# A shared ScalarE copy for q and k, a rotating pair of PSUM banks for the x transpose, and GpSimd-built sink rows in a fused attention and highway kernel

## The chip, the cores and the metric

The kernel runs on one core of one Trainium2 chip. The metric is the device time of one execution in microseconds (us). The kernel before had a median of 137.3 us when it was handed over, and of 137.55 us over four runs. The profiles show the span of one execution on the core, which is about 1.7 us shorter than the timed figure of the same run. Here "slow" means only a run that was over 1.5% above the fastest of its kernel, and all ratios use fast runs alone; a median that is quoted is over all runs of its kernel.

## The reference, cut to what matters

```python
# q, k, v: (4 batches, 8 heads, 768 positions, 64)
scores = q @ k.T / 8
keep   = (pos_k < 4) | ((pos_q - pos_k >= 0) & (pos_q - pos_k < 128))  # 4 sink rows + window of 128
a      = softmax(where(keep, scores, -1e9))
x      = (a @ v) laid out as (3072 tokens, 512)
H = max(x @ w_h, 0);  T = sigmoid(x @ w_t + b_t)
out = T * H + (1 - T) * x
```

The kernel cuts the 3072 tokens into 24 blocks of 128, six to a batch. A block's scores need the keys of the block itself and of the block before (except for a batch's first block), and, from a batch's third block on, the four sink rows. I call the work from x to out "the highway". Its two products are "the t matmuls" (x times w_t, opened by a matmul that adds the bias) and "the h matmuls" (x times w_h).

## The kernel before

The start: the columns of ones that give the softmax denominator (they hold 2.0 in the code, so that xh is half of x, which the last steps make up for) are set before the loads, for the first three v buffers, and the others inside the loop, each just before its v load is issued. All loads are issued by GpSimd and cast fp32 to fp16.

```python
def init_v(vt):
    nc.vector.memset(vt[:, 0:H * 65].rearrange("p (h e) -> p h e", e=65)[:, :, D:D + 1], 2.0)
    nc.vector.memset(vt[:, H * 65:VW], 0.0)

for vt in v_ring[0:3]:
    init_v(vt)
...
    load(0); ...; load_v(0); load(1); ...; load_v(1); ...; load(2)
    nc.gpsimd.dma_start(out=wt_sb, in_=moe_w_t...)
    load_v(2)
    load(3)
    nc.gpsimd.dma_start(out=wh_sb, in_=moe_w_h...)
```

The program uses eight PSUM banks: two score buffers of two banks each, one av buffer of two, and the pool `m_ps` with two one-bank buffers. The x transpose shares the av buffer. The q and k transposes share one bank of `m_ps`, and two engines copy them out:

```python
def stage_T(n):
    tp = m_ps.tile([P, 2 * NHP, P], FP16, tag="m", name="tp")
    ...                                            # 8 TensorE transposes
    nc.scalar.copy(out=qT, in_=tp[:, 0:NHP, :])
    nc.vector.tensor_copy(out=kT, in_=tp[:, NHP:2 * NHP, :])

def stage_X(n):
    xtp = av_ps.tile([P, NOC, P], FP16, tag="av", name="xtp")
    ...
```

The main loop (cut to its order; the program order on TensorE, VectorE and ScalarE is exactly this):

```python
for i in range(-2, NB + 1):
    s = i + 1
    stage_sink(i)        # sink scores, for two blocks at once
    stage_S(s)           # scores and exp, two halves
    stage_A(i)           # attention times v (AV), reciprocal, xh
    stage_T(i + 2)       # and, at a batch's first block, 10 small DMAs for the sink rows
    load(...); init_v(...); load_v(...)
    stage_mask(s)        # two mask multiplies
    stage_Mt(i - 1); stage_X(i); stage_Mh(i - 1)   # highway, one block behind
```

The softmax here doesn't subtract the row's maximum and nothing guards it: scores larger than these inputs give would overflow.

Of the kernel before, what the change touches and what calls it, by code (L numbers as in the profile page):

```python
# [20 lines left out]
def kernel(  # L21
# [26 lines left out]
    assert 1 <= NSINK <= 4  # L48
# [10 lines left out]
    AHEAD = 8  # L59

# [4 lines left out]
    es_pool = ctx.enter_context(tc.tile_pool(name="p_es", bufs=2))  # L65
    r_pool = ctx.enter_context(tc.tile_pool(name="p_r", bufs=3))
    x_pool = ctx.enter_context(tc.tile_pool(name="p_x", bufs=4))
# [6 lines left out]
    NV = AHEAD + 3  # L74
# [3 lines left out]
    def load(n):  # L78
        b, c = divmod(n, NSC)
        rows = slice(c * P, (c + 1) * P)  # L80
        qsd = sd_pool.tile([P, H, D], FP16, tag="qsd", name="qsd")
        ksd = sd_pool.tile([P, H, D], FP16, tag="ksd", name="ksd")
        nc.gpsimd.dma_start(out=qsd, in_=q[b, :, rows, :].transpose([1, 0, 2]))  # L83
        nc.gpsimd.dma_start(out=ksd, in_=k[b, :, rows, :].transpose([1, 0, 2]))  # L84
        qk_sd[n] = (qsd, ksd)
# [7 lines left out]

    warm = const.tile([P, DM], FP16, tag="warm")
    nc.vector.memset(warm, 0.0)
    ident = const.tile([P, P], FP16, tag="ident")
    nc.vector.memset(ident, 1.0)
    ebias = const.tile([P, 1], FP32, tag="ebias")
    nc.vector.memset(ebias, _EXP_BIAS)
    mask = const.tile([P, 2, P], FP16, tag="mask", name="mask")  # L100
    nc.vector.memset(mask, 1.0)

    def init_v(vt):

        nc.vector.memset(vt[:, 0:H * 65].rearrange("p (h e) -> p h e", e=65)[:, :, D:D + 1], 2.0)
        nc.vector.memset(vt[:, H * 65:VW], 0.0)

    for vt in v_ring[0:3]:
        init_v(vt)
    wh_sb = const.tile([P, NOC, DM], FP16, tag="wh")  # L110
    wt_sb = const.tile([P, NOC, DM], FP16, tag="wt")

    with tc.manual_schedule(engines={ENG.Pool}):
        load(0)
# [4 lines left out]
        load(1)  # L119

# [7 lines left out]
        load(2)  # L128
        nc.gpsimd.dma_start(out=wt_sb, in_=moe_w_t.rearrange("(kc p) of -> p kc of", p=P))
        load_v(2)  # L130
        load(3)
        nc.gpsimd.dma_start(out=wh_sb, in_=moe_w_h.rearrange("(kc p) of -> p kc of", p=P))


    bt32 = const.tile([1, DM], FP32, tag="bt32")
    nc.sync.dma_start(out=bt32, in_=moe_b_t.unsqueeze(0))
    bt16 = const.tile([P, DM], FP16, tag="bt16")
    nc.vector.memset(bt16, 0.0)
    ones_row = const.tile([P, P], FP16, tag="ones_row")
    nc.vector.memset(ones_row, 0.0)  # L140
    nc.vector.memset(ones_row[0:1, :], 1.0)
    mask0 = const.tile([P, P], FP16, tag="mask0", name="mask0")
    mask1 = const.tile([P, 2, P], FP16, tag="mask1", name="mask1")


    ks_bd, vs_bd = [], []
    for i in range(2):
        t = const.tile([P, NHP * 160], FP16, tag=f"ks{i}", name=f"ks{i}")
        nc.vector.memset(t, 0.0)
        ks_bd.append(t)  # L150
        t = const.tile([P, 2, 4, 65], FP16, tag=f"vs{i}", name=f"vs{i}")
        nc.vector.memset(t, 0.0)
        vs_bd.append(t)

    def warm_up(n):

        w = m_ps.tile([P, DM], FP32, tag="m", name="wps")
        for _ in range(n):
            nc.tensor.matmul(w, lhsT=warm[:, 0:P], rhs=warm, start=True, stop=True)

    def late_constants():

# [5 lines left out]


    qkT = {}  # L170
    e_of = {}
    es_of = {}
    xh_of = {}
    xT_of = {}

    def stage_T(n):
# [6 lines left out]
        qT = qkT_pool.tile([P, NHP, P], FP16, tag="qT", name="qT")  # L183
        kT = qkT_pool.tile([P, NHP, P], FP16, tag="kT", name="kT")
        nc.scalar.copy(out=qT, in_=tp[:, 0:NHP, :])  # L185
        nc.vector.tensor_copy(out=kT, in_=tp[:, NHP:2 * NHP, :])  # L186
        qkT[n] = (qT, kT)

    def stage_sink_setup(b):

        _, kT = qkT[b * NSC]
        ks3 = ks_bd[b % 2].rearrange("p (a b) -> p a b", b=160)
        for hh in range(2):
            rows = slice(64 * hh, 64 * hh + 64)
            nc.sync.dma_start(out=ks3[rows, :, 4 * hh:4 * hh + NSINK],
                              in_=kT[rows, :, 0:NSINK])
        vt = v_ring[(b * NSC) % NV]
        for h in range(H):
            r = 32 * (h // 2) + 4 * (h % 2)
            nc.sync.dma_start(out=vs_bd[b % 2][r:r + NSINK, h // 4, h % 4, :],  # L200
                              in_=vt[0:NSINK, 65 * h:65 * h + 65])

    def stage_sink(n):

        b = n // NSC
        ks = ks_bd[b % 2]
# [6 lines left out]
        es = es_pool.tile([P, 2, P], FP16, tag="es", name="es")  # L213
        nc.scalar.activation(out=es, in_=sk, func=AF.Exp, bias=ebias, scale=SCALE)
        es_of[n] = es_of[n + 1] = es

    def stage_S(n):
        c = n % NSC
        qT, kT = qkT[n]
        srcs = ([] if c == 0 else [qkT[n - 1][1]]) + [kT]  # L220
        np_ = len(srcs)
        es = []
        for g in range(2):
            sps = s_ps.tile([P, 2, 512], FP32, tag="s", name="sps")
            for hl in range(2):
                hp = 2 * g + hl
                for pc, kk in enumerate(srcs):
                    for hh in range(2):
                        rows = slice(64 * hh, 64 * hh + 64)
                        o = (hl * np_ + pc) * P  # L230
                        nc.tensor.matmul(sps[:, hh, o:o + P], lhsT=kk[rows, hp, :],  # L231
                                         rhs=qT[rows, hp, :], start=True, stop=True)
            e = e_pool.tile([P, 2, 2, np_, P], FP16, tag="e", name="e")
            nc.scalar.activation(out=e.rearrange("p a b c d -> p a (b c d)"),  # L234
                                 in_=sps[:, :, 0:2 * np_ * P], func=AF.Exp,
                                 bias=ebias, scale=SCALE)
            es.append(e)
        e_of[n] = (es, np_)

    def stage_mask(n):  # L240
        c = n % NSC
        es, np_ = e_of[n]
        m = {0: mask0, 1: mask1.rearrange("p a b -> p (a b)")}.get(
            c, mask.rearrange("p a b -> p (a b)"))
        for e in es:
            ev = e.rearrange("p a b c d -> p (a b) (c d)")
            nc.vector.tensor_tensor(  # L247
                out=ev, in0=ev, in1=m.unsqueeze(1).to_broadcast([P, 4, np_ * P]),
                op=ALU.mult)

    def stage_A(n):
        b, c = divmod(n, NSC)
        es, np_ = e_of.pop(n)
        vts = ([] if c == 0 else [v_ring[(n - 1) % NV]]) + [v_ring[n % NV]]
        av = av_ps.tile([P, 2, 4, P], FP32, tag="av", name="av")
        for g in range(2):
            first = True
            for hl in range(2):
                for hh in range(2):
                    h = 2 * (2 * g + hl) + hh  # L260
                    for pc, vt in enumerate(vts):
                        nc.tensor.matmul(  # L262
                            av[:, g, 2 * hl + hh, 0:_AVN], lhsT=es[g][:, hh, hl, pc, :],
# [3 lines left out]
            if c >= 2:  # L267
                nc.tensor.matmul(
                    av[:, g, :, 0:65], lhsT=es_of[n][:, c % 2, :],
                    rhs=vs_bd[b % 2][:, g, :, :], start=False, stop=True,  # L270
                    skip_group_check=True)
        es_of.pop(n, None)
        avh = av.rearrange("p g h e -> p (g h) e")
        rec = r_pool.tile([P, H], FP32, tag="rec", name="rec")
        nc.vector.reciprocal(out=rec.unsqueeze(2), in_=avh[:, :, 64:65])
        xh = x_pool.tile([P, H, D], FP16, tag="xh", name="xh")
        nc.vector.tensor_tensor(  # L277
            out=xh, in0=avh[:, :, 0:D],
            in1=rec.unsqueeze(2).to_broadcast([P, H, D]), op=ALU.mult)
        xh_of[n] = xh  # L280

    def stage_X(n):
        xh = xh_of[n]
        xtp = av_ps.tile([P, NOC, P], FP16, tag="av", name="xtp")
        for j in range(NOC):
            nc.tensor.transpose(xtp[:, j, :], xh[:, 2 * j:2 * j + 2, :], ident)  # L286
        xT = x_pool.tile([P, NOC, P], FP16, tag="xT", name="xT")
        nc.scalar.copy(out=xT, in_=xtp)  # L288
        xT_of[n] = xT

    u_of = {}

    def stage_Mt(n):
# [3 lines left out]
        for kc in range(NOC):  # L297
            nc.tensor.matmul(tps, lhsT=xT[:, kc, :], rhs=wt_sb[:, kc, :],  # L298
                             start=False, stop=(kc == NOC - 1))
        u = td_pool.tile([P, DM], FP16, tag="u", name="u")  # L300
        nc.scalar.activation(out=u, in_=tps, func=AF.Tanh)  # L301
        u_of[n] = u

    def stage_Mh(n):
        xT = xT_of.pop(n)
        xh = xh_of.pop(n).rearrange("p h d -> p (h d)")
        u = u_of.pop(n)
        hps = m_ps.tile([P, DM], FP32, tag="m", name="hps")
        for kc in range(NOC):
            nc.tensor.matmul(hps, lhsT=xT[:, kc, :], rhs=wh_sb[:, kc, :],  # L310
                             start=(kc == 0), stop=(kc == NOC - 1))
        dd = td_pool.tile([P, DM], FP16, tag="dd", name="dd")
        nc.vector.scalar_tensor_tensor(out=dd, in0=hps, scalar=0.0, in1=xh,  # L313
                                       op0=ALU.max, op1=ALU.subtract)
        ee = td_pool.tile([P, DM], FP16, tag="ee", name="ee")
        nc.vector.scalar_tensor_tensor(out=ee, in0=u, scalar=1.0, in1=dd,  # L316
                                       op0=ALU.add, op1=ALU.mult)
        otok = o_pool.tile([P, DM], FP32, tag="otok", name="otok")
        nc.vector.scalar_tensor_tensor(out=otok, in0=xh, scalar=2.0, in1=ee,  # L319
# [3 lines left out]
    with tc.manual_schedule(engines={ENG.PE, ENG.DVE, ENG.Activation}):  # L323
        for i in range(-2, NB + 1):
            s = i + 1
            if 0 <= i < NB and i % NSC >= 2 and i % 2 == 0:
                stage_sink(i)
            if 0 <= s < NB:
                stage_S(s)
# [60 lines left out]
```

## Time and profile before

| | kernel before |
|---|---|
| median of 4 runs | 137.55 us (136.64 to 137.91) |
| span in the profile | 134.9 us |
| first AV / third AV / last AV start | 12.82 / 25.3 / 122.7 us |
| steady period of six blocks | 28.13 us, 4.69 a block |

The profile's first part gives each engine's busy time, its share of the span, and the instruction count. PE is TensorE, PEld its weight loads, DVE VectorE, ACT ScalarE and POOL GpSimd.

```profile
PE 117.1 (87%) x1312; PEld 73.6 (55%) x1312; DVE 108.5 (80%) x230; ACT 90.4 (67%) x129; POOL 65.7 (49%) x81
```

Its second part cuts the span in 40 slices; a digit is the busy share in tenths, and the PEclk row is TensorE's granted clock in tenths.

```profile
PE   6657939999999899999999899999998999999720
DVE  6153724789988999899898998998989998999590
PEclk9999995999999999999999999999999999999996
```

The windows view of the stretch from 30 to 110 us gives its length, then the busy time of PE, PEld, DVE, ACT and POOL (instruction counts in brackets), the clock, the DMA share and GB/s.

```profile
30.00:110.00 80.00, 76.82 (x929) 49.41 (x928) 73.64 (x138) 63.04 (x92) 41.23 (x48) 1.00 1.51 143
```

So in the steady stretch TensorE is 96% busy and VectorE 92%. Which of the two sets the pace is not told by those shares, since matmuls overlap one another (the AV matmuls last 0.21 us each and start 0.05 us apart). The timeline of VectorE tells more. Its columns are start, duration, engine, line, operation, what is written from what, and the count; a bracket at the end is the idle time before and what released it. The first line here is from one batch earlier.

```profile
37.76 1.28 DVE L247 TENSOR_TENSOR e<-e,mask 128x1024 f16<-128x1024 f16 x2
...
65.55 0.42 DVE L186 COPY kT<-tp 128x512 f16<-128x512 f16 x1 [0.40 <-ACT qT L185]
65.89 1.28 DVE L247 TENSOR_TENSOR e<-e,mask 128x1024 f16<-128x1024 f16 x2
67.09 0.69 DVE L313 SCALAR_TENSOR_TENSOR dd<-hps,xh 128x512 f16<-128x512 f32 x1
67.88 0.69 DVE L316 SCALAR_TENSOR_TENSOR ee<-u,dd 128x512 f16<-128x512 f16 x1
68.61 0.69 DVE L319 SCALAR_TENSOR_TENSOR otok<-xh,ee 128x512 f32<-128x512 f16 x1
69.22 0.20 DVE L275 RECIPROCAL rec<-av 128x8 f32<-128x8 f32 x1
69.45 0.69 DVE L277 TENSOR_TENSOR xh<-av,rec 128x512 f16<-128x512 f32 x1
```

The same mask multiply starts at 37.76 and 65.89 us, which is the period of 28.13 us. Inside a block VectorE goes from one instruction to the next, apart from one wait of 0.40 to 0.45 us in three of the six blocks (for the q copy, as here, or for the h matmuls), and these lines are the budget that the change was to cut.

Three places in the timeline of TensorE: the first AV, the first sink scores with the third AV, and the last AV (v_91 and so on are buffer names).

```profile
12.82 0.93 PE L262 MATMUL av<-v_91,e 128*128 128x112 f16 x8
...
24.22 0.61 PE L211 MATMUL sk<-qT,ks_154 128*128 128x128 f16 x8
...
25.32 0.22 PE L262 MATMUL av<-v_92,e 128*128 128x112 f16 x1
...
122.69 0.21 PE L262 MATMUL av<-v_91,e 128*128 128x112 f16 x1
```

Two groups of the profile's list of costliest groups are the copies in question (total busy, mean ns of one, then idle time before them and its releaser):

```profile
L185 ACT COPY qT<-tp 128x512 f16<-128x512 f16 x24 | 14.0, 585 | 9.6 <-PE tp L182 9.6
L186 DVE COPY kT<-tp 128x512 f16<-128x512 f16 x24 | 10.1, 423 | 11.7 <-ACT qT L185 11.7
```

The k copy waits for the q copy. Both read one PSUM bank, from two engines. The Trainium skill (PSUM — Partial Sum Buffer, "PSUM bank collisions raise a hardware error") says that two engines must not touch one bank (in the same partitions) at once, readers included, and that the guard should go by bank and 32-partition quadrant, or simply by bank; here the program makes the second copy wait, and this group waited 11.7 us in all. Most of that lies at the start: in the two batches from 45 to 101 us it was 1.6 us.

### The profile page before, as it was taken

How to read it: one execution, taken by the hardware profiler on the slowest of the kernel's cores; microseconds unless marked ns; L12 is line 12 of the kernel's file. 1: busy time of each engine (PE TensorE's matmuls, PEld its weight loads, DVE VectorE, ACT ScalarE, POOL GpSimd, SP SyncE). 2: the span in 40 equal slices, each digit the busy share in tenths (PEclk: the TensorE clock that was granted, in tenths of full speed). 3: DMA queues.
4: the chain of work that ended last, by engine and by line, in shares of the span. 5: the costliest groups of instructions: out<-in, count | busy, mean ns of one | idle time of the engine just before them, and what ended most of it. 6: DMA issues, size and time to landing. Idle time of an engine off the chain costs nothing.

```text
span 134.9 us, 3378 instructions
## 1 busy us (share of the span) xinstructions
PE 117.1 (87%) x1312; PEld 73.6 (55%) x1312; DVE 108.5 (80%) x230; ACT 90.4 (67%) x129; POOL 65.7 (49%) x81
## 2 busy tenths in 40 slices
PE   6657939999999899999999899999998999999720
PEld 2225625856864466567565557656653685665300
DVE  6153724789988999899898998998989998999590
ACT  3054843779775977977777788779767977973310
POOL 6999747889897789979489370000000000000000
PEclk9999995999999999999999999999999999999996
DMA  0999999999999999999999999122011101101111
GB/s 4 111 123 127 160 188 160 155 181 171 154 198 191 196 151 148 152 195 240 192 194 179 193 194 176 38 80 80 6 78 78 63 19 78 78 5 78 78 78 78
DMA packets 81841, 17.02 MB, mean 126 GB/s; under 512 B 77729, under 2 KB 78753, under 8 KB 81826
## 3 DMA queue, kind: packets, MB, share of 16 engines
q0 software_dynamic: 75936, 10.49, 116.0%
q1 hardware_dynamic: 5890, 6.33, 14.6%
q8 instruction: 10, 0.16, 0.5%
q14 instruction: 5, 0.04, 0.1%
HBM read 20.97 MB, written 6.29 MB: 202 GB/s over the span
## 4 chain that ended last, share of the span: by engine, by line
DVE 33%; PE 32%; ACT 11%; issue 8%; POOL 7%; DMA 6%; DVEq 0%; POOLq 0%
PE hps L310 12%; ACT e L234 7%; DMA ksd<-in_k_dram 6%; DVE ee L316 6%; DVE otok L319 6%; DVE dd L313 6%; DVE e L247 5%; DVE xh L277 5%; PE tps L298 4%; PE xtp L286 4%; PE av L262 3%; DVE kT L186 3%; PE sk L211 3%; ACT qT L185 3%; POOL qsd L83 2%
## 5 line engine op out<-in xcount | busy, mean ns | idle before, releaser
L234 ACT ACTIVATE e<-sps,ebias 128x1024 f16<-128x1024 f32 (+1 forms) x48 | 47.4, 1039 | 11.2 <-PE sps L231 6.0
L298 PE MATMUL tps<-wt_sb,xT 128*128 128x512 f16 x96 | 25.5, 390 | 0.0
L310 PE MATMUL hps<-wh_sb,xT 128*128 128x512 f16 x96 | 24.7, 379 | 0.7
L83 POOL DMA_DIRECT2D qsd<-in_q_dram x24 | 21.6, 900 | 4.7 <-DMA wh_sb<-in_moe_w_h_dram 1.0
L84 POOL DMA_DIRECT2D ksd<-in_k_dram x24 | 21.4, 893 | 3.1 <-PE tp L182 1.3
L262 PEld LDWEIGHTS <-e 128*128 128x128 f16 x352 | 19.8, 98 | 3.2 <-issue 0.4
L301 ACT ACTIVATE u<-tps 128x512 f16<-128x512 f32 x24 | 14.4, 600 | 9.5 <-PE tps L298 9.5
L247 DVE TENSOR_TENSOR e<-e,mask 128x1024 f16<-128x1024 f16 x32 | 20.5, 682 | 0.0
L185 ACT COPY qT<-tp 128x512 f16<-128x512 f16 x24 | 14.0, 585 | 9.6 <-PE tp L182 9.6
L313 DVE SCALAR_TENSOR_TENSOR dd<-hps,xh 128x512 f16<-128x512 f32 x24 | 16.5, 688 | 4.1 <-PE hps L310 4.1
L186 DVE COPY kT<-tp 128x512 f16<-128x512 f16 x24 | 10.1, 423 | 11.7 <-ACT qT L185 11.7
L316 DVE SCALAR_TENSOR_TENSOR ee<-u,dd 128x512 f16<-128x512 f16 x24 | 16.6, 692 | 2.5
L319 DVE SCALAR_TENSOR_TENSOR otok<-xh,ee 128x512 f32<-128x512 f16 x24 | 16.6, 692 | 0.8
L277 DVE TENSOR_TENSOR xh<-av,rec 128x512 f16<-128x512 f32 x24 | 16.6, 691 | 0.8
L231 PE MATMUL sps<-qT,kT 64*128 64x128 f16 x352 | 15.4, 227 | 2.1 <-DVE kT L186 1.1
L231 PEld LDWEIGHTS <-kT 64*128 64x128 f16 x352 | 10.7, 98 | 9.5 <-issue 6.6
L288 ACT COPY xT<-xtp 128x512 f16<-128x512 f16 x24 | 14.0, 583 | 1.1 <-PE xtp L286 0.9
L298 PEld LDWEIGHTS <-xT 128*128 128x128 f16 x96 | 9.6, 100 | 9.1 <-issue 0.8
L310 PEld LDWEIGHTS <-xT 128*128 128x128 f16 x96 | 9.3, 98 | 8.6 <-issue 1.5
L286 PEld LDWEIGHTS <-xh 128*128 128x128 f16 x96 | 6.4, 101 | 13.4 <-DVE xh L277 11.2
L286 PE MATMUL xtp<-ident,xh 128*128 128x128 f16 x96 | 9.9, 228 | 3.8 <-DVE xh L277 3.8
L180 PE MATMUL tp<-ident,qsd 128*128 128x128 f16 x96 | 10.0, 231 | 2.4 <-DMA qsd<-in_q_dram 2.3
(88 smaller groups left out, 152.9 us busy)
## 6 DMA issues: line engine op xcount, KB each, us to landing
out_dram<-otok SPq DMA_DIRECT2D x24, 256.0 KB
qsd<-in_q_dram POOLq DMA_DIRECT2D x24, 128.0 KB, 7.3
ksd<-in_k_dram POOLq DMA_DIRECT2D x24, 128.0 KB, 7.4
wt_sb<-in_moe_w_t_dram POOLq DMA_DIRECT2D x1, 512.0 KB, 8.4
wh_sb<-in_moe_w_h_dram POOLq DMA_DIRECT2D x1, 512.0 KB, 10.1
v_91<-in_v_dram POOLq DMA_DIRECT2D x3, 128.0 KB, 8.0
v_92<-in_v_dram POOLq DMA_DIRECT2D x3, 128.0 KB, 6.1
v_93<-in_v_dram POOLq DMA_DIRECT2D x2, 128.0 KB, 8.0
```

What stands on the lines that cost most here:

```text
L83: nc.gpsimd.dma_start(out=qsd, in_=q[b, :, rows, :].transpose([1, 0, 2]))
L231: nc.tensor.matmul(sps[:, hh, o:o + P], lhsT=kk[rows, hp, :], rhs=qT[rows, hp, :], start=True, stop=True)
L234: nc.scalar.activation(out=e.rearrange("p a b c d -> p a (b c d)"), in_=sps[:, :, 0:2 * np_ * P], func=AF.Exp, bias=ebias, scale=SCALE)
L247: nc.vector.tensor_tensor(out=ev, in0=ev, in1=m.unsqueeze(1).to_broadcast([P, 4, np_ * P]), op=ALU.mult)
L262: nc.tensor.matmul(av[:, g, 2 * hl + hh, 0:_AVN], lhsT=es[g][:, hh, hl, pc, :], rhs=vt[:, 65 * h:65 * h + _AVN], start=first, stop=False, ...
L277: nc.vector.tensor_tensor(out=xh, in0=avh[:, :, 0:D], in1=rec.unsqueeze(2).to_broadcast([P, H, D]), op=ALU.mult)
L286: nc.tensor.transpose(xtp[:, j, :], xh[:, 2 * j:2 * j + 2, :], ident)
L298: nc.tensor.matmul(tps, lhsT=xT[:, kc, :], rhs=wt_sb[:, kc, :], start=False, stop=(kc == NOC - 1))
L310: nc.tensor.matmul(hps, lhsT=xT[:, kc, :], rhs=wh_sb[:, kc, :], start=(kc == 0), stop=(kc == NOC - 1))
L313: nc.vector.scalar_tensor_tensor(out=dd, in0=hps, scalar=0.0, in1=xh, op0=ALU.max, op1=ALU.subtract)
L316: nc.vector.scalar_tensor_tensor(out=ee, in0=u, scalar=1.0, in1=dd, op0=ALU.add, op1=ALU.mult)
L319: nc.vector.scalar_tensor_tensor(out=otok, in0=xh, scalar=2.0, in1=ee, op0=ALU.mult, op1=ALU.add)
```

## The change

The intent: take work from VectorE (the k copy moves into one 1024-wide ScalarE copy), reorder VectorE's instructions so that dependent ones don't stand next to each other, take the x transpose out of the av buffer so that the next AV needn't wait for it, run the highway two blocks behind so that its inputs are always ready, and replace ten small DMAs per batch for the sink rows by GpSimd work (two copies for k, and for v a multiply that is fed by one small load). The diff cut to its core (long renamings into one function per engine are left out):

```diff
-    NV = AHEAD + 3
+    LAG = 2
+    NV = AHEAD + 4
 ...
+        load_qk(2)
+        ...                                  # two selects that build bm, the head pattern
+        load_v(2)
+        load_sink_v(0)
+        load_qk(3)
+        load_v(3)
         nc.gpsimd.dma_start(out=wt_sb, in_=moe_w_t...)
-        load_v(2)
-        load(3)
         nc.gpsimd.dma_start(out=wh_sb, in_=moe_w_h...)
+        load_qk(4)
+        load_v(4)
 ...
-        nc.scalar.copy(out=qT, in_=tp[:, 0:NHP, :])
-        nc.vector.tensor_copy(out=kT, in_=tp[:, NHP:2 * NHP, :])
+        qk = qkT_pool.tile([P, 2 * NHP, P], FP16, tag="qk", name="qk")
+        nc.scalar.copy(out=qk, in_=tp_of.pop(n))
 ...
-            nc.sync.dma_start(out=ks3[rows, :, 4 * hh:4 * hh + NSINK], in_=kT[rows, :, 0:NSINK])
+            nc.gpsimd.tensor_copy(out=dst[:, :, 4 * hh:4 * hh + NSINK], in_=kT[rows, :, 0:NSINK])
-        for h in range(H):                   # v sink rows, 8 DMAs
-            nc.sync.dma_start(out=vs_bd[...][...], in_=vt[0:NSINK, 65 * h:65 * h + 65])
+        nc.gpsimd.tensor_tensor(out=vs_bd[b % 2][0:NS4, :, 0:D], in0=vs_dn..., in1=bm..., op=ALU.mult)
 ...
-        xtp = av_ps.tile([P, NOC, P], FP16, tag="av", name="xtp")
+        xtp = m_ps.tile([P, NOC, P], FP16, tag="m", name="xtp")
```

The new loop, with the checks for the ends cut away:

```python
for i in range(-2, NB + LAG + 1):
    m, o = i - LAG, i - LAG - 1
    if i == -2:
        warm_up(8); more_constants(); late_constants()
        for vt in v_ring[3:NV]: init_v(vt)          # after the loads of v blocks 3 and 4 are issued
        sink_ones(); sink_v(0)
    act_sink(i); pe_S(i + 1, 0); act_S(i + 1, 0); pe_S(i + 1, 1)
    dve_d(o); dve_mask(i, 1)
    pe_T(i + 2); pe_X(i - 1); dve_e(o); pe_A(i)
    act_T(i + 2); act_X(i - 1)
    act_S(i + 1, 1); dve_mask(i + 1, 0); dve_rec(i); dve_o(o); dve_x(i)
    pe_Mt(m); act_u(m); pe_Mh(m); pe_sink(i + 1)
    for n in ((5 .. AHEAD) if i == -2 else (i + 2 + AHEAD)): load_qk(n); load_v(n)
    if (i + 2) % NSC == 0: pool_sink((i + 2) // NSC)   # k sink copies, on GpSimd, behind the loads
    if i % NSC == 3: load_sink_v(i // NSC + 1)
    if i % NSC == 0 and i > 0: sink_v(i // NSC)
```

## The prediction

> **What bounds the kernel now.** In steady state VectorE. The timeline repeats every 28.13 us per batch of six blocks (mask multiplies at 37.84, 65.97, 94.11), 4.69 us per block. The windows view from 30 to 110 us gives VectorE 92% busy, TensorE 96% (pipelined, not its limit), ScalarE about 79%. Start to start on VectorE: k copy 0.34, masks 1.20, dd 0.79, ee 0.73, otok 0.61, reciprocal 0.23, xh 0.6: about 4.5. Start-up is loads: block 3 is transposed at 19.5, the third block's attention-times-v (AV) starts at 25.3, the last block's AV at 122.7, and the span ends at 134.9.
>
> **Removed, added, moved, per block.**
> - VectorE loses the k copy (0.34) and, by interleaving dd/mask/ee/mask/reciprocal/otok/xh, some 0.4 of dependent-instruction gaps: about 3.8.
> - ScalarE: one 128x1024 copy for a 128x512 one. The exp goes from 684 to 1110 ns between 512 and 1024 columns, 0.83 ns each, as the Trainium skill (ScalarE: Activation LUTs, What ACT_TABLE_LOAD costs) has it; so the 585 ns copy becomes an estimated 1.01 us. ScalarE about 3.9.
> - TensorE: the same work, about 4.2 by starts in the timeline. Now the busiest.
> - The two-bank rotation makes a new loop: highway h matmuls 0.86, first score half 0.41, its exp 1.0, the q/k copy 1.01, then the t matmuls (they need that copy's bank) 1.07: 4.4 us; about 5.0 where the sink scores stand in it, 3.9 around a batch's first block. I estimate 4.2 to 4.6 a block, middle 4.45. Over 21 blocks this gains about 5 us.
>
> **New at the start, on the critical path.** The wait list of the built program shows that the ones-columns of v blocks 3 and 4 are now set after their loads were issued, so these two small memsets wait for the loads to land. They stand before every mask on VectorE. Block 4's v follows both weight matrices; the same load was issued at 18.6 before and took 7.2 to 8.1 us, so I put its landing at 26 us, and the first block's AV at about 28 (before: 12.8). Then GpSimd: block 5's v load waits for a memset behind the same stall, and ten load issues of 0.89 us precede the k sink copies, which the third block's sink scores need: about 36. The third block's AV comes at about 37, 12 us later than before. The last block's tail grows by about 1.3 us (one block more lag).
>
> **Sum.** 37.4 + 21x4.45 = 130.9 for the last AV, plus 13.4 for AV, tail and store: 144 us span. The timed median was 2.4 above the profile's span: about 146 us.
>
> Predicted 145 us, range 138 to 151. Faster by over 2%: 0.08; within 2%: 0.16; slower by over 2%: 0.76.
>
> **What would show it.** Timeline: no mask multiply before about 25 us, VectorE's wait there put down to the load of v block 4; the first sink-score matmul waiting on GpSimd until about 36. Timeline from 50 to 110 us: period under 4.69; waits: TensorE's t matmuls waiting on the ScalarE q/k copy; VectorE under 90% busy. No k copy on VectorE; the ScalarE copy near 1.0 us.
>
> **What would make it wrong.** The stalls being shorter (loads landing by 20 us because nothing else is queued), which alone gives about 139; a TensorE-bound period of 4.2 or less, worth another 5 us; both together would make it slightly faster. A period at 4.7 would put it near 150.

## The result, and the profile after

The changed kernel is correct and slower: a median of 153.46 us (152.95 to 153.79, four runs) against 137.55 us for the kernel before. The ratio is 1.119, with a 95% interval of 1.112 to 1.126. Ratios are from the fast runs of the two kernels in the same rounds, so they are not quite the ratio of the medians quoted. The span of the profiled run is 151.2 us. The predicted direction was right, but the time was above the predicted range (138 to 151).

Where the 16.3 us of span came from, by the start of the third and the last block's AV matmuls in the two timelines:

| stretch | before | after | difference |
|---|---|---|---|
| start to third AV | 25.3 | 40.80 | +15.5 |
| third AV to last AV (21 blocks) | 97.4 | 95.8 | -1.5 |
| last AV to end | 12.2 | 14.6 | +2.4 |

The stream of blocks did become a little faster. Nearly all the loss is at the start. The busy line and the slices of the changed kernel:

```profile
PE 116.1 (77%) x1312; PEld 75.9 (50%) x1312; DVE 96.4 (64%) x213; ACT 98.6 (65%) x129; POOL 74.8 (49%) x99
```

```profile
PE   6555000390999998999999989999998999998840
DVE  6220000553157978777977878877799777798691
PEclk9999999999599999999999999999999999999999
```

A slice is 3.8 us. Counted from one, TensorE does nothing in slices 5 to 7 (15 to 26 us), works in slices 8 and 9, and stops again in slice 10 (34 to 38 us). VectorE, at 8 and 9 tenths before, is at 7 and 8. The costliest-groups list has the new copy, and a group that was not worth a look before: a memset that costs 65 ns and stood idle for 19.2 us in all.

```profile
L206 ACT COPY qk<-tp 128x1024 f16<-128x1024 f16 x24 | 24.0, 1001 | 7.0 <-PE tp L201 7.0
L94 DVE MEMSET v<- 128x8 f16 x12 | 0.7, 65 | 19.2 <-DMA v<-in_v_dram 19.2
```

**The first stop.** The timeline of VectorE in the changed kernel:

```profile
17.74 0.07 DVE L94 MEMSET v<- 128x8 f16 x1 [8.93 <-DMA v<-in_v_dram]
...
28.09 0.07 DVE L94 MEMSET v<- 128x8 f16 x1 [10.26 <-DMA v<-in_v_dram]
...
28.60 1.34 DVE L265 TENSOR_TENSOR e<-e,mask 128x512 f16<-128x512 f16 x3
```

The ones columns of v blocks 3 and 4 lie in the same buffers that the loads fill, and their loads were issued first. So these two memsets wait until the loads have landed, and start at 17.74 and 28.09 us. The load of block 4 stands behind both weight matrices. Every mask multiply is behind the memsets on VectorE, and every AV needs a mask: the first AV starts at 29.06 us, and at 12.82 before.

**The second stop.** The timelines of GpSimd and of TensorE in the changed kernel:

```profile
20.35 0.92 POOL L84 DMA_DIRECT2D ksd<-in_k_dram  x1
28.51 0.88 POOL L91 DMA_DIRECT2D v<-in_v_dram  x1 [7.24 <-DVE v L94]
...
36.30 0.96 POOL L91 DMA_DIRECT2D v<-in_v_dram  x1
37.17 0.54 POOL L215 COPY ks<-qk 64x16 f16<-64x16 f16 x2
```

```profile
29.06 0.93 PE L280 MATMUL av<-v,e 128*128 128x112 f16 x8 [15.56 <-DVE e L265]
...
37.77 0.87 PE L224 MATMUL sk<-qk,ks 128*128 128x128 f16 x8 [3.92 <-POOL ks L215]
...
40.80 0.85 PE L280 MATMUL av<-v,e 128*128 128x112 f16 x8
...
136.64 0.56 PE L280 MATMUL av<-v,e 128*128 128x112 f16 x8
```

Block 5's v load waits for its own ones column, which stands behind the stalled memsets. Then GpSimd issues ten loads, 0.86 us apart, before it comes to the two k sink copies at 37.17 us. The first sink scores need those rows. The Trainium skill (TensorE: Matmul & The Clock Gate, "Part 1: The HAM clock gate") says that TensorE's clock drops after about 3.4 us of idleness. This trace agrees: after the 3.92 us wait the eight sink matmuls took 0.87 us, where the kernel before takes 0.61 for the same group (the first of the eight start 56 to 66 ns apart, the last 107), and slice 11 of the clock row shows a 5. (The eight AV matmuls after the first stop took 0.93 us, and take 0.56 in the steady state, though the clock row has a 9 there. That is not the stop: the first eight of the kernel before took 0.93 us too, with no such stop ahead of them, and the changed kernel's x transposes still took 0.63 us at 31.72 and 0.39 at 45.15. TensorE ran slowly from the start, and the row does not show that.) So the path from the sink copies to the third AV at 40.80 runs at a low clock.

**The steady state.** One batch's masks to the next batch's are 27.83 us, so 4.64 us a block instead of 4.69 (timeline of VectorE in the changed kernel):

```profile
83.46 0.42 DVE L265 TENSOR_TENSOR e<-e,mask 128x512 f16<-128x512 f16 x1
...
111.29 0.42 DVE L265 TENSOR_TENSOR e<-e,mask 128x512 f16<-128x512 f16 x1
```

VectorE is no longer the limit: it is busy 56.5 of the 70 us from 60 to 130. What binds now is shown by one block in the timelines of TensorE and of ScalarE:

```profile
85.68 0.62 PE L246 MATMUL sps<-qk 64*128 64x128 f16 x16
...
88.19 0.38 PE L319 MATMUL tps<-bt,ones_row 128*128 128x512 f16 x1 [0.71 <-ACT qk L206]
...
89.26 1.03 PE L334 MATMUL hps<-wh_sb,xT 128*128 128x512 f16 x4
90.22 0.62 PE L246 MATMUL sps<-qk 64*128 64x128 f16 x16
```

```profile
86.12 1.11 ACT L254 ACTIVATE e<-sps,ebias 128x1024 f16<-128x1024 f32 x1 [0.60 <-PE sps L246]
87.13 1.00 ACT L206 COPY qk<-tp 128x1024 f16<-128x1024 f16 x1
```

Read them as one ring: the score matmuls start at 85.68, their exp at 86.12, the q and k copy right after it on ScalarE at 87.13, and then the t matmuls at 88.19, which wait for that copy because they need its PSUM bank; the h matmuls follow at 89.26, and the next block's scores at 90.22. That is 4.54 us, in which every step waits for the one before. The last link holds beyond this block: from 58 to 92 us the t matmuls start 0.05 us after the end of the q and k copy in six cases of seven, and 0.09 us after it in the seventh. It is what the prediction had called a new loop. As long as the t matmuls stand on it, taking work from VectorE can't shorten the period.

### The profile page after: what moved, and what is told of

It is laid out like the page before. It is cut to its first block, busy times and chain, and to the rows that moved or that the text cites. A ratio compares the mean times of both kernels' runs of the same rounds, so it can differ in the third digit from the quotient of the medians.

```text
span 151.2 us, 3275 instructions
## 1 busy us (share of the span) xinstructions
PE 116.1 (77%) x1312; PEld 75.9 (50%) x1312; DVE 96.4 (64%) x213; ACT 98.6 (65%) x129; POOL 74.8 (49%) x99
## 4 chain that ended last, share of the span: by engine, by line
PE 47%; ACT 19%; POOL 14%; DMA 7%; issue 6%; DVE 4%; POOLq 0%; DVEq 0%
PE hps L334 13%; PE tps L321 13%; ACT qk L206 10%; ACT e L254 9%; DMA v<-in_v_dram 7%; PE tps L319 5%; PE sps L246 4%; POOL qsd L83 4%; POOL v L91 4%; POOL ksd L84 4%; PE av L280 3%; PE sk L224 3%; DVE dd L340 2%; PE tp L199 2%; PE xtp L308 2%
## 5 line engine op out<-in xcount | busy, mean ns | idle before, releaser
L254 ACT ACTIVATE e<-sps,ebias 128x1024 f16<-128x1024 f32 (+1 forms) x48 | 50.2, 1046 | 22.6 <-PE sps L246 22.4
L280 PE MATMUL av<-v,e 128*128 128x112 f16 x352 | 24.7, 220 | 16.2 <-DVE e L265 16.2
L265 DVE TENSOR_TENSOR e<-e,mask 128x1024 f16<-128x1024 f16 (+1 forms) x48 | 30.6, 640 | 5.8 <-ACT e L254 5.1
L280 PEld LDWEIGHTS <-e 128*128 128x128 f16 x352 | 21.5, 102 | 16.9 <-DVE e L265 16.7
L83 POOL DMA_DIRECT2D qsd<-in_q_dram x24 | 22.3, 928 | 13.4 <-PE tp L201 12.6
L206 ACT COPY qk<-tp 128x1024 f16<-128x1024 f16 x24 | 24.0, 1001 | 7.0 <-PE tp L201 7.0
L91 POOL DMA_DIRECT2D v<-in_v_dram x24 | 22.1, 922 | 7.5 <-DVE v L94 7.2
L246 PE MATMUL sps<-qk 64*128 64x128 f16 x352 | 15.6, 231 | 2.2 <-ACT qk L206 2.2
L321 PEld LDWEIGHTS <-xT 128*128 128x128 f16 x96 | 9.3, 97 | 15.9 <-issue 7.1
L246 PEld LDWEIGHTS <-qk 64*128 64x128 f16 x352 | 11.0, 100 | 9.4 <-issue 7.3
L352 DVE SCALAR_TENSOR_TENSOR otok<-xh,ee 128x512 f32<-128x512 f16 x24 | 15.6, 651 | 0.1
L334 PEld LDWEIGHTS <-xT 128*128 128x128 f16 x96 | 9.4, 98 | 11.3
L94 DVE MEMSET v<- 128x8 f16 x12 | 0.7, 65 | 19.2 <-DMA v<-in_v_dram 19.2
L319 PE MATMUL tps<-bt,ones_row 128*128 128x512 f16 x24 | 9.1, 378 | 4.5 <-ACT qk L206 3.1
```

The source lines that it names most:

```text
L83: nc.gpsimd.dma_start(out=qsd, in_=q[b, :, rows, :].transpose([1, 0, 2]))
L91: nc.gpsimd.dma_start(out=vt[:, :, 0:D], in_=v[b, :, rows, :].transpose([1, 0, 2]))
L206: nc.scalar.copy(out=qk, in_=tp_of.pop(n))
L246: nc.tensor.matmul(sps[:, hh, o:o + P], lhsT=kk[rows, hp, :], rhs=qT[rows, hp, :], start=True, stop=True)
L254: nc.scalar.activation(out=e.rearrange("p a b c d -> p a (b c d)"), in_=sps[:, :, 0:2 * np_ * P], func=AF.Exp, bias=ebias, scale=SCALE)
L265: nc.vector.tensor_tensor(out=ev, in0=ev, in1=m.unsqueeze(1).to_broadcast([P, 4, np_ * P]), op=ALU.mult)
```

## The experiments

Fifteen kernels were run, in five calls. Times are compared with the runs of the kernel before; where an excess over it is quoted, it is the difference of the two medians. Kernels are compared only within the same rounds. All give right results unless said otherwise. Of the runs of these kernels one each of v4_before_weights and all_three was slow, and is left out of the ratios, though not of the medians.

### Call 1: the start

The theory was that the start is lost by two orders, each of which can be undone alone: the ones columns behind the loads, and the sink copies behind ten load issues. The rival was that the start is lost to the loads (block 4's v behind the weights).

**init_first**: set the ones columns of v blocks 3 and 4 before the loads.

```diff
-        for vt in v_ring[0:3]:
+        for vt in v_ring[0:5]:
             init_v(vt)
 ...
-                for vt in v_ring[3:NV]:
+                for vt in v_ring[5:NV]:
                     init_v(vt)
```

> The ones-columns of v blocks 3 and 4 are set before their loads are issued; nothing else differs from the changed kernel. Theory (the two memsets hold VectorE until v block 4 has landed at 28.1 us): first mask multiply before 13 us, first AV at about 13 instead of 29.1. But the k sink copies on GpSimd still stand behind twelve load issues, some of which wait for earlier loads to land, so the third block's AV comes at about 35 instead of 41.0: 147 us, 6 us less than the changed kernel. Rival (the loads themselves, not the memsets, set the start: block 4's q and k land at about 27 whatever VectorE does): first AV early, but the time within 2 us of 153.5.

Measured 148.77 us, 12.2 above the kernel before (136.59); ratio 1.090 [1.083, 1.097]. The first AV came at 13.67 us instead of 29.06, but the sink scores then waited far longer. In the timeline of TensorE:

```profile
33.40 1.03 PE L224 MATMUL sk<-qk,ks 128*128 128x128 f16 x8 [13.91 <-POOL ks L215]
```

**sink_early**: issue the sink copies before the loads of the same turn of the loop.

```diff
+            if on(i + 2) and (i + 2) % NSC == 0:
+                pool_sink((i + 2) // NSC)
             first, last = (5, AHEAD) if i == -2 else (i + 2 + AHEAD, i + 2 + AHEAD)
             for n in range(first, last + 1): ...
-            if on(i + 2) and (i + 2) % NSC == 0:
-                pool_sink((i + 2) // NSC)
```

> The k sink copies stand ahead of the loads of blocks 5 to 8 on GpSimd; the memset stall is left in. Theory: the first sink-score matmul no longer waits for GpSimd until 37.7; first AV still at 29, third block's AV at about 35.5 instead of 41.0, TensorE's clock not reduced there: about 148 us. Rival (the sink wait is hidden by the loads of block 3 and 4): under 1 us gained.

Measured 147.54 us, 11.0 above; ratio 1.079 [1.070, 1.087]. The copies ran at 19.43, the first AV still came late (27.14), and the third AV at 33.62 instead of 40.80.

**init_sink**: both edits.

> Both edits together. Theory: then only the loads bound the start: TensorE transposes block 4 ahead of the third block's AV, and block 4's k lands at about 27, so that AV starts at about 28 instead of 41.0: 140 to 141 us, 13 us less than the changed kernel and still 2% slower than the kernel before, because the steady state is only 0.05 us a block shorter and the tail longer. If the two stalls did not add to what the single edits give, the sum of the single gains (11 us) would be missed.

Measured 141.22 us, 4.6 above; ratio 1.038 [1.030, 1.045]. The sink scores in the timeline of TensorE, now with almost no wait and at full clock:

```profile
20.02 0.62 PE L224 MATMUL sk<-qk,ks 128*128 128x128 f16 x8 [0.35 <-POOL ks L215]
```

The changed kernel is 15.9 above the kernel before. One edit alone brings 3.7 of that back, the other 5.0, and both 11.3. Each delay had hidden part of the other. The two orders are thus shown to be the cause of 11.3 of the 15.9 us.

**v4_before_weights**: the rival; only the order of the loads is changed.

```diff
+        load_qk(4)
+        load_v(4)
         nc.gpsimd.dma_start(out=wt_sb, in_=moe_w_t...)
         nc.gpsimd.dma_start(out=wh_sb, in_=moe_w_h...)
-        load_qk(4)
-        load_v(4)
```

> Only the order of loads: block 4's q, k and v ahead of the two weight matrices; memsets and sink copies as in the changed kernel. Theory: v block 4 lands some 6 us earlier (at about 21 to 22), VectorE is released then, GpSimd reaches the sink copies about 9.6 us later (31), third block's AV at about 34; the t matmuls wait a little for their weights. About 147 us. Rival (VectorE waits for something else, or for all loads): VectorE's first mask multiply stays at 28 us.

Measured 149.47 us, 12.9 above; ratio 1.095 [1.087, 1.103]. VectorE came free at 20.50 us and the first AV at 21.47, but the sink copies still stood behind the load issues, some of which now waited for the weights. The timeline of GpSimd:

```profile
27.24 0.88 POOL L84 DMA_DIRECT2D ksd<-in_k_dram  x1 [1.59 <-DMA wh_sb<-in_moe_w_h_dram]
...
32.19 0.49 POOL L215 COPY ks<-qk 64x16 f16<-64x16 f16 x2
```

The load order matters, but it treats the delay and doesn't remove it; I had expected 147.

### Call 2: the loop

The theory was the loop of banks above. The rival was that TensorE's or ScalarE's own work sets 4.64 us.

**x_before_qk**: put the x transpose and its copy ahead of the q and k transposes and copy, on TensorE and on ScalarE, so that the t matmuls take the bank of the x copy.

```diff
-            if on(i + 2):
-                pe_T(i + 2)
             if on(i - 1):
                 pe_X(i - 1)
+            if on(i + 2):
+                pe_T(i + 2)
 ...
-            if on(i + 2):
-                act_T(i + 2)
             if on(i - 1):
                 act_X(i - 1)
+            if on(i + 2):
+                act_T(i + 2)
```

> Transpose of x ahead of the transpose of q and k, on TensorE and for the two copies on ScalarE; nothing else. Then the t matmuls take the bank that the short x copy frees, and the h matmuls the one of the q/k copy. Theory (the loop h matmuls, first score half, exp, q/k copy, t matmuls bounds the steady state at 4.54 us, 5.03 with sink scores): the loop falls to about 4.15, TensorE's own work of 4.2 a block takes over, period of six blocks 27.83 to about 25.6 us: 153.5 to about 146 us. Rival (TensorE is simply full, 96% busy): period unchanged within 0.3 us per six blocks.

Measured 150.14 us, 12.9 above the kernel before (137.22); ratio 1.099 [1.091, 1.108]. The period fell to 27.12 us, not to the 25.6 expected. The direction was right; something else binds just below the loop.

**x_copy_first**: only the two copies are swapped on ScalarE (the second half of the diff above).

> Only the order of the two copies on ScalarE is turned round (x copy ahead of the q/k copy); TensorE's order stays, so the t matmuls still wait for the bank of the q/k copy. Same work on every engine. Theory (bank loop): the loop gets longer by the x copy, 0.5 us a block, period of six blocks 27.8 to about 30.5 us: about 163 us. Rival (TensorE full, or ScalarE's total load): no change within 1%.

Measured 150.94 us; ratio 1.104 [1.098, 1.110]; period 26.90 us. I had expected it to lengthen the loop, and it did the opposite. The trace explains why: from 58 to 92 us the t matmuls start 0.05 to 0.23 us after the end of the x copy, and over 3 us after that of the q and k copy. With the x copy first, they get the bank of the x copy; the pool does not hand out its two buffers by turns. (I read from the built program that it hands out the one that was released first; no run here shows that rule.) So this edit, too, took the loop away. The list of waits from 45 to 137 us (engine, line, what it waited for; total us, times, longest) has for the changed kernel, and then for x_copy_first:

```profile
PE tps L319 <- ACT qk L206: 3.1, 6, 0.7
```

```profile
PE tps L319 <- ACT xT L313: 0.9, 3, 0.3
```

The wait on the q and k copy is gone. It was 3.1 us in about 20 blocks, so 0.93 us in six, and the period fell by 27.83 - 26.90 = 0.93 us. That the two are equal is chance: waits of about 0.1 us are not in the list, and x_copy_first has the new wait of the second line. The wait that the list shows is small, because in the loop nearly every step is work; the ring of starts showed it, not the size of the wait.

**two_copies**: q copied by ScalarE and k by VectorE again, to see whether ScalarE's longer copy is what costs.

```diff
-        nc.scalar.copy(out=qk, in_=tp_of.pop(n))
+        nc.scalar.copy(out=qk[:, 0:NHP, :], in_=tp_of[n][:, 0:NHP, :])
+    def dve_T(n):
+        nc.vector.tensor_copy(out=qk_of.pop(n)[:, NHP:2 * NHP, :], in_=tp_of.pop(n)[:, NHP:2 * NHP, :])
```

> q is copied by ScalarE and k by VectorE again, in the changed order. The built program makes the k copy wait for the q copy (same bank), so they still follow each other: 0.58 + 0.42 us against 1.00. Theory (bank loop): no gain, period within 0.1 us a block of 4.64, time 152 to 156, although ScalarE has 0.42 us a block less to do. Rival (ScalarE's load, 86% busy in the steady state, bounds it): period 0.3 to 0.4 us a block shorter, about 146 us.

Measured 153.13 us; ratio 1.120 [1.112, 1.129]; period 28.05 us. ScalarE lost about 0.42 us of work a block and the period did not fall, so ScalarE's total work is not the limit. The second copy waits for the first, but that is not what holds the t matmuls here: the edit also changed who gets which bank, and they wait for the x copy (list of waits, 45 to 137 us):

```profile
DVE qk L212 <- ACT qk L207: 4.1, 9, 0.6
PE tps L324 <- ACT xT L318: 3.6, 7, 0.8
```

From 58 to 92 us the t matmuls start 0.05 us after the end of the x copy in every block. That copy stands behind the q copy on ScalarE, and from the start of the exp to its end it is 2.07 us (85.88 to 87.95), where the changed kernel has 2.01 to the end of its one copy (86.12 to 88.13). So the ring stayed as long with another copy in it, and the run does not tell what an earlier release of the q and k bank is worth.

**all_three**: init_sink with x_before_qk.

> Early memsets, early sink copies and x ahead of q and k. Theory: 13 us from the start and 7 from the steady state: about 133.5 us, about 3% faster than the kernel before. If the start is load-bound more than I think, 135 to 137.

Measured 140.06 us, 2.8 above; ratio 1.022 [1.014, 1.031]. I had expected 133.5. Two things were left over: a start that is bound by loads, and one step of 7.21 us at block 8 (between two blocks' xh). There the second batch's first sink product waits for the GpSimd fill of the v sink rows, which stands behind load issues (timeline of TensorE):

```profile
58.14 0.27 PE L286 MATMUL av<-vs,es 128*128 128x260 f16 x1 [2.06 <-POOL vs L129]
```

### Call 3: the limit of the loop, and of the kernel before

**forced_bank**: x_copy_first again, but with two pools of one buffer each instead of one pool of two, so that the t matmuls must take the bank of the q and k copy, as I had believed of x_copy_first.

```diff
-    m_ps = ctx.enter_context(tc.tile_pool(name="ps_m", bufs=2, space=bass.MemoryType.PSUM))
+    m_ps = ctx.enter_context(tc.tile_pool(name="ps_m", bufs=1, space=bass.MemoryType.PSUM))
+    n_ps = ctx.enter_context(tc.tile_pool(name="ps_n", bufs=1, space=bass.MemoryType.PSUM))
-        xtp = m_ps.tile([P, NOC, P], FP16, tag="m", name="xtp")
+        xtp = n_ps.tile([P, NOC, P], FP16, tag="n", name="xtp")
-        hps = m_ps.tile([P, DM], FP32, tag="m", name="hps")
+        hps = n_ps.tile([P, DM], FP32, tag="n", name="hps")
 ...                       # and the two ScalarE copies swapped, as in x_copy_first
```

> The x copy goes ahead of the q/k copy on ScalarE as in the run before, where the built program shows that the pool then gave the t matmuls the x copy's bank (it hands out the bank that was released first), so that run had taken the loop away instead of lengthening it. Here each bank is a pool of its own: q/k, t and sink share one, x and h the other. So the t matmuls wait for the q/k copy again, which now comes 0.5 us later. Work on every engine as in the changed kernel. Theory (bank loop): six blocks take about 30.5 us instead of 27.83 (26.90 with the other bank), about 162 us. Rival (the loop is not what bounds; the order of the copies as such made the gain): 26.9 to 27.8 us, 150 to 153 us.

Measured 163.18 us; ratio 1.197 [1.189, 1.205]; period 30.99 us, with 30.5 expected. The list of waits from 45 to 137 us:

```profile
PE tps L320 <- ACT qk L207: 12.8, 18, 1.2
```

The program order on every engine is the same as in x_copy_first; only the banks differ. The period went from 26.90 to 30.99 us. This is the most direct evidence that the bank handed to the t matmuls sets the pace. (The h and the sink-score matmuls changed banks with them, but the list has no wait of theirs.)

**x_copy_first_no_bias**: wrong (relative error 0.51); the bias matmul is removed from x_copy_first, to see whether TensorE is the next limit.

```diff
-        nc.tensor.matmul(tps, lhsT=ones_row, rhs=bt16, start=True, stop=False)
 ...
-                             start=False, stop=(kc == NOC - 1))
+                             start=(kc == 0), stop=(kc == NOC - 1))
```

> Wrong result on purpose: the bias matmul of 0.22 us a block is left out; the order with the x copy first, where the t matmuls no longer wait for the q/k copy. Theory (TensorE's own work is what is left there): six blocks from 26.90 to about 25.6 us, the whole about 4.5 us shorter. Rival (another wait bounds it): unchanged within 0.3 us per six blocks.

Measured 146.97 us; ratio 1.078 [1.070, 1.085]; period 26.10 us. It fell by 0.80 of the 1.29 us that six bias matmuls take (six starts of 0.215 us). Four of the six blocks shrank by about 0.2 us each and two did not. So the bias matmul is on the path in four blocks of six. That does not make TensorE's own work the limit in all four. In x_copy_first it is so in two: their t matmuls (at 74.38 and 83.55 us) start with TensorE idle for no time and 0.22 us after the x copy has ended. In the other two (at 64.88 and 87.66) they start 0.05 us after its end, which is a shorter ring of the same kind, through the x copy, of 4.11 us. The two blocks that did not shrink are those with sink scores, whose matmuls start about 0.05 us after the end of ScalarE's tanh of the t product, in both kernels (at 67.30 us in x_copy_first, at 65.72 here). These readings are from the traces and were not tested.

**before_no_bias**: wrong; the same removal in the kernel before.

> Wrong result on purpose: the kernel before without the bias matmul. Theory (VectorE with its gaps bounds the steady state of the kernel before): six blocks stay at 28.13 us within 0.3, time within 1%. Rival (TensorE bounds that too, 96% busy): about 26.8 us per six blocks, 4.5 us less.

Measured 137.39 us; ratio 1.009 [1.002, 1.017]; period 28.18 us against 28.13, so not shorter. (The whole was 0.9% longer with a matmul less in each block; in the profile the third AV starts at 25.83 us instead of 25.32, which I did not follow up.) TensorE was not the limit of the kernel before, although its busy share was 96%. This agrees with the Trainium skill (Perfetto Trace Analysis, "Identifying the Most-Contended Engine"), which warns that matmul busy time judges TensorE badly.

**mended**: init_sink, x_copy_first, LAG 1, the v sink fill moved to an earlier turn and ahead of the loads, and the AV of blocks 1 and 2 put ahead of the transposes of blocks 3 and 4 (in init_sink TensorE had waited there for block 4's loads with an AV ready behind).

```diff
-    LAG = 2
+    LAG = 1
 ...
-            if on(i + 2):
+            if on(i + 2) and i not in (1, 2):
                 pe_T(i + 2)
 ...
             if on(i):
                 pe_A(i)
+            if i in (1, 2):
+                pe_T(i + 2)
 ...
+            if i >= 0 and i % NSC == 5 and i // NSC + 1 < B:
+                sink_v(i // NSC + 1)
```

> The changed kernel with early memsets, early k and v sink fills, the x copy first, a lag of one block, and the attention-times-v of blocks 1 and 2 ahead of the transposes of blocks 3 and 4. Theory: fourth block's xh at about 31, six blocks 26.9 us, tail 2 us shorter than the changed kernel's: about 132.5 to 134 us, 2.5 to 3.5% faster than the kernel before. If the loads bound the first blocks more than I think: 136.

Measured 137.08 us against 136.61; ratio 1.007 [0.999, 1.014]: a tie. The period was 26.91 us, but the start was now waiting for the weights, as the load order of the change puts them behind v block 3 (timeline of TensorE):

```profile
22.75 1.87 PE L321 MATMUL tps<-wt_sb,xT 128*128 128x512 f16 x4 [3.75 <-DMA wt_sb<-in_moe_w_t_dram]
```

### Calls 4 and 5: a version that beats both

**mended_old_loads**: mended with the load order of the kernel before.

```diff
         load_qk(2)
         ...
+        nc.gpsimd.dma_start(out=wt_sb, in_=moe_w_t...)
         load_v(2)
         load_sink_v(0)
         load_qk(3)
-        load_v(3)
-        nc.gpsimd.dma_start(out=wt_sb, in_=moe_w_t...)
         nc.gpsimd.dma_start(out=wh_sb, in_=moe_w_h...)
+        load_v(3)
```

> The mended kernel with the loads in the order of the kernel before (t weights ahead of block 3, h weights ahead of v block 3). In the mended kernel TensorE stood 3.8 us for the t weights (22.7) and then for the h weights (25.1) with the third block's sink scores behind them. Theory (the rest of the start is this load order): t weights by about 18, fourth block's xh at about 31.5 instead of 35.9, steady state 26.9 us per six blocks, tail as in the mended kernel: 133 us, 3% faster than the kernel before. Rival (the start is bound by the sum of the bytes, whatever their order): 136 to 137.

Measured 134.58 us against 136.70; ratio 0.985 [0.980, 0.989]. One step at block 8 took 6.59 us, since the GpSimd fill of the v sink rows waited 2.27 us for its small load.

**mended_lag2**: mended with LAG 2 instead of 1.

> The mended kernel with a lag of two, so that no highway matmul stands ahead of the third block's sink scores; loads in the changed kernel's order. Theory: third block's AV at about 22, fourth block's xh at about 31.5 (block 4's k lands at 27), tail 2 us longer than with lag one: about 135 us, 1 to 1.5% faster than the kernel before. Rival (sum of the bytes): no better than 137.

Measured 136.44 us against 136.70; ratio 0.999 [0.994, 1.004]. With the late weights, two blocks of lag are no worse than one (mended was 1.007): the longer tail and the weights' wait seem to weigh about the same, which I have not taken apart.

**mended_early_vd**: mended_old_loads, with that small load issued three turns earlier.

```diff
-            if i >= 0 and i % NSC == 3 and b < B:
+            if i >= 0 and i % NSC == 0 and b < B:
                 load_sink_v(b)
```

> As the mended kernel with the old load order, but each batch's small v-sink load is issued three blocks earlier, so that GpSimd's fill does not wait for it (2.3 us there, and TensorE 1.5 us behind it at block 8). Theory: the 6.59 us step at block 8 falls back to 4.99: 1.6 us less, 133 us, 2.5 to 3% faster than the kernel before. Rival (GpSimd is behind with its load issues there, whatever the small load does): unchanged at 134.6.

Measured 133.80 us (six runs, 132.76 to 134.44) against 137.17; ratio 0.974 [0.968, 0.979]. The step at block 8 is back at 4.99 us, the period is 26.91 us and the span 132.5 us. This version is 2.6% faster than the kernel before, and it keeps the change's one copy, its VectorE order, its PSUM pools and its GpSimd sink rows; only other orders and the lag differ. Its busy line:

```profile
PE 115.6 (87%) x1312; PEld 75.1 (57%) x1312; DVE 96.3 (73%) x213; ACT 98.5 (74%) x129; POOL 75.0 (57%) x99
```

The busy times are those of the changed kernel to within 1 us on every engine, and the span is 18.7 us shorter: the whole difference is waiting.

## Why the prediction was right or wrong

**Right as far as tested: what bounded the kernel before.** It named VectorE. Removing a matmul from each block left the period at 28.18 us, which rules out TensorE. That VectorE itself is the limit was read from its timeline, where it goes without a wait through three blocks of six and waits 0.40 to 0.45 us in the others; no kernel was run that took work from VectorE alone.

**Right: the mechanism at the start, with both links.** It foresaw that the memsets would wait for v block 4, that no mask would run before about 25 us (28.60 measured), that ten load issues would stand ahead of the sink copies, and that the sink scores would wait on GpSimd. The experiments that undid the two orders gave back 11.3 of 15.9 us.

**Right: the new loop, VectorE's relief and the copy's duration.** The copy was estimated at 1.01 us from the slope of the exp, as the skill's page on ScalarE has it, and took 1.00 in the trace. VectorE fell to 81% busy (under 90% predicted). The t matmuls wait on the q and k copy, and x_copy_first and forced_bank show that the bank they get sets the pace.

**Wrong: the size, by 6.9 us of span.** The sum was 37.4 + 93.5 + 13.4 = 144.3 us, and the span was 151.2. The added 2.4 us from span to timed median came out (2.3 measured, 153.46 - 151.2), in part by luck: the profiled run's own time is only 1.75 us above its span, and that run was the fastest of the four. The terms that failed:

| term of the sum | predicted | measured | off by |
|---|---|---|---|
| third AV starts | 37.4 | 40.80 | +3.4 |
| 21 blocks to the last AV | 93.5 (4.45 each) | 95.8 (4.56 each) | +2.3 |
| last AV to the end | 13.4 | 14.6 | +1.2 |

1. "The third block's AV comes at about 37". This is the largest part of the miss. Block 4's v was put at 26 us, from loads that took up to 8.1 us in the kernel before, and landed at 28.0, as it took 10.5 us from its issue at 17.53, behind the two weight matrices. The profile before could have told: there v block 3, issued at 13.42 right behind the h weights, landed at 23.86, after 10.4 us; the 8.1 us came from a load issued 5 us later. The sink rows were put at about 36 and were ready for TensorE at 37.77. From there to the third AV the sum left 1.4 us, and it took 3.0, because TensorE had idled and ran at a low clock; the prediction had no term for that, though it had foreseen the idle time.
2. "I estimate 4.2 to 4.6 a block, middle 4.45." The steady period was 4.64. First, the middle was lower than its own terms: weighed as they occur in a batch (three blocks of 4.4, two with sink scores of 5.0, one of 3.9), they give 4.52. Second, the ring of a plain block was 4.54 by starts, and the terms add up to 4.35: from the bias matmul to the next scores it took 2.03 us (1.93 predicted), from the q and k copy to the t matmuls 1.06 (1.01), from the scores to their exp 0.44 (0.41), and the exp 1.01 (1.0). Each term was short by a little, and in a ring they add up.
3. "The last block's tail grows by about 1.3 us". It grew by 2.4. The second half of the last AV now waits 0.65 us for its mask multiply (it starts 1.32 us after the first half, and 0.50 before), for which the sum had no term; the rest was not taken apart.

All three terms were too small and none too large. The range was narrow for a sum of terms that were each read from an undisturbed stretch, and then used for a disturbed one.

**Wrong beside the number: what the period falls to without the loop.** x_before_qk and x_copy_first took the loop away and stopped at 27.12 and 26.90 us, 4.5 a block, with the bias matmul on the path of four blocks of six, and TensorE without idle time in two of these. Taking the waits of TensorE (1.2 us by starts) out of one period of x_copy_first leaves some 4.3 us a block as TensorE's own work, an estimate, where the prediction had 4.2. The "TensorE-bound period of 4.2 or less", named as a way to be wrong, was reached by none of these runs.

## What to carry to other kernels

A small setup instruction on a buffer that a load fills must be issued before the load: issued after it, it waits for the landing, and in an in-order queue so does everything behind it (65 ns of memset cost 19.2 us of idle VectorE here). When two delays stand one behind the other, undoing either alone shows little (3.7 and 5.0 us, but 11.3 together), so undo them together before judging either. When buffers rotate through few banks, follow who gets the bank of whom and add up the ring of starts: here one swap of two copies moved the period by 0.93 us, and with the other bank assignment the same swap moved it by 3.2 us the other way, with no instruction added.

## What the Trainium skill lacked or had wrong

- ScalarE: Activation LUTs, "What ACT_TABLE_LOAD costs": its form for immediate operands (186 ns plus 0.833 ns per element) would give 612 and 1039 ns for copies of 512 and 1024 columns; an estimate from that page. Measured were 585 and 1001 ns, some 4% less; these copies read PSUM, and the page doesn't say where its tile lay, so this need not be a contradiction. The slope of 0.81 ns that these two give (416 ns over 512 columns) is close to the page's.
- DMA: Bandwidth & Descriptors, "Latency and other measured facts" and the section on the anatomy of one DMA: it has a first-byte latency of about 1 us for loads issued from GpSimd, but no figure for how long an issue holds GpSimd's own queue. Here each casting 128x512 load held it for 0.88 to 0.96 us, so that ten of them put the copy behind them off by 8.7 us (28.51 to 37.17). The page's fit (2.0 us plus bytes over 436 GB/s) gives 2.3 us for 128 KB, an estimate; these loads took a median of 4.6 to 5.3 us from issue to landing, and the one behind the weights 10.5 us, all of them with other loads in flight.
- Perfetto Trace Analysis, "Identifying the Most-Contended Engine": it advises to read the weight-load share (and a share of peak FLOPs, which I did not work out) instead of the matmul share. The weight-load share does not tell these two states apart. The share was 62% in the kernel before, where removing a matmul changed nothing, and 65% in x_copy_first, where it shortened four blocks of six. The windows view of x_copy_first from 60 to 130 us, to be set beside that of the kernel before:

```profile
60.00:130.00 70.00, 67.94 (x842) 45.56 (x840) 58.84 (x110) 63.23 (x85) 26.28 (x33) 1.00 0.92 107
```

- No page says how a PSUM tile pool picks among its buffers; in x_copy_first it does not go by turns. This is a matter of software, but it decided two experiments: 26.90 us a period with the pool's choice, 30.99 us with the banks fixed.
